# Loading q and k in 2-KB pieces and turning them with 64x64 products: chunked attention and a cosine router on one Trainium2 core

## The chip, the cores and the metric

The kernel runs on one core of one Trainium2 chip. The metric is the device time of one execution in microseconds (us); less is better. The time before is the median of three executions. A separate execution was profiled, and every line of a profile below comes from it.

## What is computed

Everything is in 32-bit floating point. The first part is attention within chunks of 64 tokens, for 8 batches, 8 heads, 576 tokens (9 chunks) and a head width of 64:

```python
q_c = q.reshape(B, H, nc, 64, D); k_c, v_c = ...
scores = matmul(q_c, k_c.transpose(0, 1, 2, 4, 3)) / sqrt(D)
attn = exp(scores - max(scores))
attn = attn / (sum(attn) + 1e-9)
out = matmul(attn, v_c)
```

Its result, 4608 tokens of 512 numbers (the 8 heads side by side), goes into a mixture of 8 experts. A router takes the cosine of each token with 8 expert vectors, divides it by tau, and sends the token to the best expert alone, with the softmax weight of that expert as a gate:

```python
logits = normalised(x) @ normalised(expert_emb).T / tau
e = argmax(logits); g = softmax(logits)[e]
out = g * (relu(x @ w1[e]) @ w2[e])        # w1: 512 x 1024, w2: 1024 x 512
```

## The kernel before

**Two parts.** The first part does attention and routing, and writes each token's row, with its place number, square sum and gate, to a table in DRAM (`spots`) at a place sorted by expert. The second part reads that table in blocks of 128 rows and runs the two layers of the experts (`hidden_part`, `result`, L196 to L250). The change touches the first part alone. It ends some 205 us into the execution.

**Tiles and rounds.** The first part works on 36 tiles of 128 tokens, that is two chunks each. A tile passes through stages: `load_qk`, `turn_qk`, `scores`, `weights`, `turn_a`, `values`, `turn_x`, `logits`, and for each four tiles `copy_logits`, `pick`, `gates`, `place` and `put`. The loop at L779 is a software pipeline whose order is written out by hand (`manual_schedule`): in the round t it emits `turn_a(t)`, `turn_qk(t+3)`, `load_qk(t+7)`, `logits(t-2)`, `scores(t+2)`, `turn_x(t-1)`, `values(t)` and `weights(t+2)`. Each engine runs its own instructions in the order in which they were emitted; semaphores between the engines do the rest. So on TensorE (PE) a round is: turn a, turn k and q, logits, scores, turn x, values.

**Loading and turning q and k.** `load_qk` (L358) brings a tile of k and of q into SBUF with one token per partition and the 8 heads side by side, 512 numbers. In DRAM the heads of a token are not neighbours, so a piece of the transfer is one head of one token, 64 numbers or 256 bytes. Tiles that lie across two batches take two transfers. q is issued by GpSimd (POOL); k by SyncE (SP) for the first four tiles and by POOL for the others. Four buffers each let the loads run four rounds ahead. `turn_qk` (L387) turns 128x128 blocks, each two heads wide, with PE's transpose into a PSUM bank: four for k, four for q. The bank of k is copied to SBUF by ScalarE (ACT, L395), that of q by VectorE (DVE, L397). The result holds the head width on partitions, even heads on the lower 64, odd ones on the upper 64, with 128 tokens along the row.

**PSUM.** The pool `ps_t` has three buffers of one bank. `turn_a`, the turn of k, the turn of q and `turn_x` take them in turn, four in a round. `scores` (L408) and `values` (L448) have two banks each of their own, and multiply by quadrants: the 64 rows of an even or odd head, against the 64 columns of one chunk or the other.

**Other names.** ACT's work in a round is the copy of aT (L436), of kxT (L395), of xT (L479), a square sum (L482) and the exponential (L428). DVE's is the copy of qxT, the maximum (L416), the subtraction (L418), and dividing by the sum (L456 to L459), which writes the token rows `xr`; there are eight buffers of these. `put` (L611) sends a row tile to `spots` with an indirect transfer issued by POOL. `load_v` (L376) brings v of a batch, 256 bytes a piece, in eight transfers on SP; the first half of batch 0 is issued by POOL.

Of the kernel before, what the change touches and what calls it, by code (L numbers as in the profile page):

```python
# [9 lines left out]
FP32 = mybir.dt.float32  # L10
# [8 lines left out]
P = 128  # L19
CH = 64  # L20
# [5 lines left out]
def kernel(  # L26
# [11 lines left out]
    nc = tc.nc  # L38
    B, H, S, Dh = q.shape
# [3 lines left out]
    NPAIR = H // 2  # L43
# [215 lines left out]
    with (  # L259
# [97 lines left out]

        def load_qk(t):  # L358

            for src, nm, eng in (  # L360
                (k, "kx", nc.sync if t < 4 else nc.gpsimd),
                (q, "qx", nc.gpsimd),
            ):
                x = qk_p.tile([P, H, Dh], FP32, tag=nm, name=nm)
                done = 0
                while done < P:
                    b, s = divmod(t * P + done, S)
                    n = min(P - done, S - s)
# [4 lines left out]
                    done += n  # L373
                qk_t[nm, t] = x.rearrange("p h d -> p (h d)")
# [12 lines left out]
        def turn_qk(t):  # L387
            for nm in ("kx", "qx"):
                a = qk_t.pop((nm, t))
                ps = ps_t.tile([P, NPAIR, P], FP32, tag="tr", name="tr")  # L390
                for i in range(NPAIR):
                    nc.tensor.transpose(ps[:, i], a[:, i * P : i * P + P], ident)  # L392
                x = wk.tile([P, NPAIR, P], FP32, tag=nm + "T", name=nm + "T")
                if nm == "kx":
                    nc.scalar.copy(x, ps)  # L395
# [532 lines left out]
```

## Time and profile before

| what | value |
|---|---|
| time, median of 3 | 737.42 us (736.25 to 737.46) |
| span of the profiled execution | 732.1 us |
| PE busy | 687.4 us, 94% |
| DVE, ACT, POOL busy | 235.2, 175.9, 167.8 us |
| mean granted clock of TensorE | 0.977 |
| DMA moved | 132.60 MB in 106,929 packets |
| packets under 512 bytes | 50,516 |

The profile names engines: PE is the matrix product, PEld its weight load, and each product in 32-bit floating point stands in it as two loads and two products. A line such as L392 is a line of the kernel; `tr<-ident,kx` names the tiles written and read; `128x512 f32` is partitions by elements. "Idle before" is the time for which the engine had nothing, and the name after the arrow is what ended it. Engines overlap, so busy times don't add up to the span: what counts is which engine has no hole in the stretch that one looks at. PE can be busy and yet not at its peak, since the profile shows a product until its results have come out.

### The profile page before, as it was taken

The page shows a single profiled execution, that of the slowest core. Times are in us where ns is not written, and L with a number is a line of the kernel's source. Part 1 is how long each engine was busy: PE and PEld are TensorE (multiplying, and loading weights), DVE is VectorE, ACT ScalarE, POOL GpSimd, SP SyncE. Part 2 cuts the span into 40 slices and gives each one's busy share as a digit, 9 for nine tenths or more (in the row PEclk, how much of TensorE's full clock was granted, in tenths as well). Part 3 has the DMA queues.
Part 4 walks back from the last instruction along what each step waited for, and adds up shares of the span by engine and source line. Part 5 has one row for each costly group of instructions (what it writes and reads, how often), then busy time and mean ns, then how long its engine had stood idle before and what let it go on. Part 6 is the DMA issues. An engine that isn't in the chain of part 4 may idle for free.

```text
span 732.1 us, 24309 instructions
## 1 busy us (share of the span) xinstructions
PE 687.4 (94%) x10327; PEld 466.1 (64%) x10327; DVE 235.2 (32%) x571; ACT 175.9 (24%) x342; POOL 167.8 (23%) x243
## 2 busy tenths in 40 slices
PE   4789999898979999999999999998999999999995
PEld 3679898797734555545545545544577777777761
DVE  2468887777553121211211211211121121121100
ACT  3356666555301111111111111111111111111110
POOL 7637776762440000001001001000000000010010
PEclk9899999899899999999999999999999999999998
DMA  9999999998946711115785416788751264411340
GB/s 199 202 185 191 255 237 241 207 230 296 351 136 246 266 54 43 36 42 201 254 324 178 162 44 219 274 323 313 273 199 43 75 233 157 151 46 41 135 165 20
DMA packets 106929, 132.60 MB, mean 181 GB/s; under 512 B 50516, under 2 KB 70996, under 8 KB 106816
## 3 DMA queue, kind: packets, MB, share of 16 engines
q1 hardware_dynamic: 94800, 93.31, 42.6%
q0 software_dynamic: 11984, 37.67, 18.2%
q8 instruction: 83, 1.36, 0.8%
q14 instruction: 30, 0.25, 0.1%
q10 hardware_dynamic: 32, 0.02, 0.0%
HBM read 341.13 MB, written 21.73 MB: 496 GB/s over the span
## 4 chain that ended last, share of the span: by engine, by line
issue 47%; PE 34%; DMA 9%; POOL 5%; DVE 4%; POOLq 0%; ACT 0%; DVEq 0%; ACTq 0%
PE h_ps L212 13%; PE y_ps L232 11%; DMA spots<-xr,dest 5%; POOL out_dram L241 3%; PE rt_ps L489 2%; DMA qx<-in_q_dram 2%; PE tr L477 2%; PE tr L392 2%; PE pv L448 2%; PE sc L408 2%; PE tr L434 1%; DMA xin<-spots 1%; DMA v<-in_v_dram 1%; DVE xr L459 1%; POOL qx L369 1%
## 5 line engine op out<-in xcount | busy, mean ns | idle before, releaser
L212 PE MATMUL h_ps<-w,xbT 128*32 128x256 f32 x4736 | 276.8, 380 | 6.6 <-issue 3.9
L232 PE MATMUL y_ps<-w,hT 128*32 128x512 f32 x2368 | 274.0, 594 | 3.5 <-DMA w<-in_moe_w_dram 2.6
L212 PEld LDWEIGHTS h_ps<-w,xbT 128*32 128x32 f32 x4736 | 203.1, 110 | 77.8 <-issue 15.1
L232 PEld LDWEIGHTS y_ps<-w,hT 128*32 128x32 f32 x2368 | 118.6, 110 | 133.4 <-issue 88.8
L222 DVE STREAM_TRANSPOSE hT<-h 128x512 f32<-128x512 f32 x74 | 52.6, 711 | 413.8 <-ACT h L221 412.7
L241 POOL DMA_INDIRECT out_dram<-y,spot x37 | 36.0, 972 | 471.7 <-ACT y L240 444.4
L221 ACT ACTIVATE h<-h_ps 128x512 f32<-128x512 f32 x74 | 44.3, 598 | 217.6 <-PE h_ps L212 217.6
L240 ACT ACTIVATE y<-y_ps,spot 128x512 f32<-128x512 f32 x37 | 25.4, 687 | 238.5 <-PE y_ps L232 219.6
L611 POOL DMA_INDIRECT spots<-xr,dest x36 | 37.4, 1039 | 45.5 <-issue 24.2
L188 DVE STREAM_TRANSPOSE xbT<-xin 128x256 f32<-128x256 f32 x74 | 43.2, 621 | 0.1
L489 PEld LDWEIGHTS rt_ps<-enT,xT 128*128 128x128 f32 x288 | 36.4, 198 | 3.7 <-DVE full L597 2.4
L489 PE MATMUL rt_ps<-enT,xT 128*128 128x8 f32 x288 | 36.3, 253 | 2.3 <-DVE full L597 2.1
L479 ACT COPY xT<-tr 128x512 f32<-128x512 f32 x36 | 21.1, 586 | 61.2 <-PE tr L477 54.6
L369 POOL DMA_DIRECT2D qx<-in_q_dram x40 | 34.4, 863 | 5.5 <-PE tr L392 2.6
L369 POOL DMA_DIRECT2D kx<-in_k_dram x36 | 31.6, 881 | 14.6 <-PE tr L392 14.2
L392 PE MATMUL tr<-ident,qx 128*128 128x128 f32 x144 | 24.5, 298 | 8.2 <-DMA qx<-in_q_dram 8.2
L392 PE MATMUL tr<-ident,kx 128*128 128x128 f32 x144 | 24.7, 299 | 7.2 <-DMA kx<-in_k_dram 6.4
L448 PE MATMUL pv<-v,aT 64*64 64x65 f32 x1152 | 28.9, 238 | 2.5 <-issue 2.4
L397 DVE COPY qxT<-tr 128x512 f32<-128x512 f32 x36 | 24.5, 681 | 17.6 <-PE tr L392 17.5
L408 PE MATMUL sc<-kxT,qxT 64*64 64x64 f32 x1152 | 27.9, 238 | 1.6 <-issue 1.5
L416 DVE TENSOR_REDUCE mx<-sc 128x8 f32<-128x512 f32 x36 | 24.7, 687 | 12.3 <-PE sc L408 9.0
L448 PEld LDWEIGHTS pv<-v,aT 64*64 64x64 f32 x1152 | 23.0, 146 | 8.2 <-issue 8.2
(140 smaller groups left out, 389.8 us busy)
## 6 DMA issues: line engine op xcount, KB each, us to landing
w<-in_moe_w_dram SPq DMA_DIRECT2D x142, 2048.0 KB
xin<-spots SPq DMA_DIRECT2D x160, 64.0 KB
qx<-in_q_dram POOLq DMA_DIRECT2D x32, 256.0 KB
v<-in_v_dram SPq DMA_DIRECT2D x56, 144.0 KB
kx<-in_k_dram POOLq DMA_DIRECT2D x28, 256.0 KB
w<-in_moe_w_dram ACTq DMA_DIRECT2D x2, 2048.0 KB
spot<-spots SPq DMA_DIRECT2D x80, 4.0 KB
spots<-blank SPq DMA_DIRECT2D x2, 528.0 KB
```

The lines of the kernel that those rows point to most:

```text
L188: nc.vector.transpose(xT[:, :, cols].rearrange("p c (b i) -> p b c i", i=Q), t[:, s * (D // 2) : (s + 1) * (D // 2)].rearrange("p (b i c) ...
L212: nc.tensor.matmul(ps[Q * r : Q * r + Q, b].rearrange("p (k i) -> p k i", i=Q), lhsT=d["xT"][:, c, t0 : t0 + Q], rhs=w[:, c, r], start=(c ...
L221: nc.scalar.activation(h, ps, AF.Relu)
L222: nc.vector.transpose(hT[:, :, G * s : G * s + G].rearrange("p k (b i) -> p b k i", i=Q), h.rearrange("p b (k i) -> p b k i", i=Q),)
L232: nc.tensor.matmul(ps[Q * r : Q * r + Q], lhsT=d["hT"][:, c, Q * r : Q * r + Q], rhs=w2_sb[r // 2][buf_of(j)][:, c], start=(c == 0), stop= ...
L241: ins = nc.gpsimd.indirect_dma_start(out=out, out_offset=bass.IndirectOffsetOnAxis(ap=spot[:, j, TOK : TOK + 1].bitcast(I32), axis=0), in_ ...
L369: eng.dma_start(out=x[done : done + n], in_=src[b, :, s : s + n, :].rearrange("h p d -> p h d"),)
L392: nc.tensor.transpose(ps[:, i], a[:, i * P : i * P + P], ident)
L408: nc.tensor.matmul(sc[CH * c : CH * c + CH, par, i], lhsT=qx[r0 : r0 + CH, i, c0 : c0 + CH], rhs=kx[r0 : r0 + CH, i, c0 : c0 + CH], start= ...
L448: nc.tensor.matmul(pv[CH * c : CH * c + CH, par, i], lhsT=d["aT"][r0 : r0 + CH, i, CH * c : CH * c + CH], rhs=v_t[b][r0 : r0 + CH, i, cb, ...
L489: nc.tensor.matmul(rt_ps[:, batch_of[t][0] % 2, batch_of[t][1]], lhsT=d["xT"][:, c], rhs=enT[:, c], start=(c == 0), stop=(c == KD - 1),)
L611: ins = nc.gpsimd.indirect_dma_start(out=spots, out_offset=bass.IndirectOffsetOnAxis(ap=at, axis=0), in_=m, in_offset=None, bounds_check=S ...
```

## The change

q and k are loaded with one head and eight neighbouring tokens per partition. Eight tokens of a head are neighbours in DRAM, so a piece is 8 x 64 numbers, or 2 KB, instead of 256 bytes; there are an eighth as many of them. A tile's two chunks are two transfers, 64 partitions each (8 heads by 8 groups of eight tokens). All k loads are issued by SP, and all of v too.

The layout in SBUF is now such that partition (h, g) holds the tokens 8g to 8g + 7 of head h. The turn takes one of the eight tokens at a time: 64 partitions by 64 numbers are the stationary operand, and 32 columns of the unit matrix, those of the even or the odd heads, are the moving one. The product puts the head width on partitions and (pair of heads, g) along the row, on the lower or upper 64 partitions for even or odd heads. For each of k and q that makes 8 tokens x 2 x 2 chunks = 32 products. A PSUM bank belongs to a chunk and holds k in its first half and q in its second. The copies to SBUF put the tokens back in order, and there are two for k and two for q, one from each bank. What later stages read is as before. The aim is to relieve the DMA engines of small pieces.

```diff
-            for src, nm, eng in (
-                (k, "kx", nc.sync if t < 4 else nc.gpsimd),
-                (q, "qx", nc.gpsimd),
-            ):
-                x = qk_p.tile([P, H, Dh], FP32, tag=nm, name=nm)
...
+            for src, nm, eng in ((k, "kx", nc.sync), (q, "qx", nc.gpsimd)):
+                x = qk_p.tile([P, H * Dh], FP32, tag=nm, name=nm)
+                for c in range(2):
+                    b, cb = divmod(2 * t + c, NCB)
                     eng.dma_start(
-                        out=x[done : done + n],
-                        in_=src[b, :, s : s + n, :].rearrange("h p d -> p h d"),
+                        out=x[CH * c : CH * c + CH],
+                        in_=src[b, :, CH * cb : CH * cb + CH, :].rearrange(
+                            "h (g j) d -> h g (j d)", j=H
+                        ),
                     )
...
         def turn_qk(t):
-            for nm in ("kx", "qx"):
+
+            banks = [
+                ps_t.tile([P, 2, 8, NPAIR, 8], FP32, tag="tr", name="tr") for c in range(2)
+            ]
+            for n, nm in enumerate(("kx", "qx")):
                 a = qk_t.pop((nm, t))
-                ps = ps_t.tile([P, NPAIR, P], FP32, tag="tr", name="tr")
-                for i in range(NPAIR):
-                    nc.tensor.transpose(ps[:, i], a[:, i * P : i * P + P], ident)
+                for j in range(8):
+                    for par in range(2):
+                        for c in range(2):
+                            r = slice(CH * c, CH * c + CH)
+                            nc.tensor.matmul(
+                                banks[c][CH * par : CH * par + CH, n, j],
+                                lhsT=a[r, j * Dh : j * Dh + Dh],
+                                rhs=ident[r, r].rearrange("p (i r g) -> p r i g", r=2, g=8)[:, par],
+                                start=True,
+                                stop=True,
+                            )
                 x = wk.tile([P, NPAIR, P], FP32, tag=nm + "T", name=nm + "T")
-                if nm == "kx":
-                    nc.scalar.copy(x, ps)
-                else:
-                    nc.vector.tensor_copy(x, ps)
+                for c in range(2):
+                    to = x[:, :, CH * c : CH * c + CH].rearrange("p i (g j) -> p i g j", j=8)
+                    came = banks[c][:, n].rearrange("p j i g -> p i g j")
+                    if nm == "kx":
+                        nc.scalar.copy(to, came)
+                    else:
+                        nc.vector.tensor_copy(to, came)
                 qkT[nm, t] = x
...
-        load_v(0, 0, 4, nc.gpsimd)
+        load_v(0, 0, 4)
```

More of the change, by code (lines that the diff above doesn't have):

```diff
@@ L358, in load_qk @@
         def load_qk(t):
-            for src, nm, eng in (
-                (k, "kx", nc.sync if t < 4 else nc.gpsimd),
-                (q, "qx", nc.gpsimd),
-            ):
-                x = qk_p.tile([P, H, Dh], FP32, tag=nm, name=nm)
[L365 to L368, printed above, removed]
+            for src, nm, eng in ((k, "kx", nc.sync), (q, "qx", nc.gpsimd)):
+                x = qk_p.tile([P, H * Dh], FP32, tag=nm, name=nm)
+                for c in range(2):
+                    b, cb = divmod(2 * t + c, NCB)
                     eng.dma_start(
-                        out=x[done : done + n],
-                        in_=src[b, :, s : s + n, :].rearrange("h p d -> p h d"),
-                    )
-                    done += n
-                qk_t[nm, t] = x.rearrange("p h d -> p (h d)")
+                        out=x[CH * c : CH * c + CH],
+                        in_=src[b, :, CH * cb : CH * cb + CH, :].rearrange(
+                            "h (g j) d -> h g (j d)", j=H
+                        ),
+                    )
+                qk_t[nm, t] = x
         def load_v(b, c0=0, c1=NCB, eng=nc.sync):
```

## The prediction

> **What bounds the kernel now.** I read the busy slices first, then stretches of the attention stage, then one round on PE and one on ACT, then the waits.
>
> ```profile
> PE   4789999898979999999999999998999999999995
> PEclk9899999899899999999999999999999999999998
> DMA  9999999998946711115785416788751264411340
> DMA packets 106929, 132.60 MB, mean 181 GB/s; under 512 B 50516, under 2 KB 70996, under 8 KB 106816
> ```
> One slice is 18.3 us. Slices 1 to 11 are attention and routing, from slice 12 on PE is full with the experts, which the change leaves alone. In slices 1 to 9 the DMA engines are full as well: half of all packets are under 512 bytes.
>
> ```profile
> 55.00:73.00 18.00, 17.94 (x370) 16.54 (x368) 14.63 (x42) 11.75 (x27) 12.75 (x18) 1.00 0.99 191
> 128.00:146.00 18.00, 15.77 (x326) 13.91 (x322) 13.60 (x38) 9.00 (x21) 12.69 (x18) 0.91 1.07 207
> ```
> Columns: PE, PEld, DVE, ACT, POOL busy, clock, DMA share, GB/s. In a good stretch PE is the bound; in a bad one it idles 2 us and loses clock.
>
> ```profile
> 65.00 0.69 PE L408 MATMUL sc<-kxT,qxT 64*64 64x64 f32 x32
> 65.62 0.66 PE L477 MATMUL tr<-ident,xr 128*128 128x128 f32 x4
> 66.21 0.69 PE L448 MATMUL pv<-v,aT 64*64 64x65 f32 x32
> 66.84 0.66 PE L434 MATMUL tr<-ident,a 128*128 128x128 f32 x4
> 67.33 0.60 PE L392 MATMUL tr<-ident,kx 128*128 128x128 f32 x4
> 67.76 0.60 PE L392 MATMUL tr<-ident,qx 128*128 128x128 f32 x4
> 68.20 0.96 PE L489 MATMUL rt_ps<-enT,xT 128*128 128x8 f32 x8
> 69.09 0.33 PE L408 MATMUL sc<-kxT,qxT 64*64 64x64 f32 x5
> ```
> One undisturbed round of a tile: 69.09 - 65.00 = 4.09 us with no hole. The two L392 turns take 0.44 us each. Over the stage a round takes more: L436 starts at 21.2 us (tile 0) and 180.7 (tile 33), 33 rounds of 4.83 us; these are the rounds that matter, since the round of tile t turns q and k of tile t + 3, and there is none to turn after tile 32. So 33 x 0.74 = 24 us are lost to waits and to half clock.
>
> ```profile
> 66.32 0.58 ACT L479 COPY xT<-tr 128x512 f32<-128x512 f32 x1 [0.87 <-PE tr L477]
> 66.80 0.63 ACT L482 ACTIVATE junk<-xr 128x512 f32<-128x512 f32 x1
> 67.33 0.19 ACT L482 ACTIVATION_READ_ACCUMULATOR junk<-xr 128x1 f32 x1
> 67.42 0.62 ACT L428 ACTIVATE a<-a 128x512 f32<-128x512 f32 x1
> 67.94 0.57 ACT L436 COPY aT<-tr 128x512 f32<-128x512 f32 x1
> 68.41 0.59 ACT L395 COPY kxT<-tr 128x512 f32<-128x512 f32 x1
> ```
> ACT does six things a round, in order, without a hole once L477's bank is there; the kx copy is the last. Now nobody waits for it soon: its reader is the L408 of the next round.
>
> ```profile
> POOL xr L465 <- DMA spots<-xr,dest: 13.5, 6, 4.8
> DVE xr L459 <- DMA spots<-xr,dest: 7.4, 5, 2.3
> ```
> What the full DMA costs: token rows leave late (us, times, longest), their buffers come free late.
>
> **What the Trainium skill says.** "PSUM — Partial Sum Buffer", section "PSUM bank collisions raise a hardware error": two engines on one bank and 32-partition quadrant collide even at other columns, so bank users must be ordered. The old program gives kx and qx a bank each, so no row of the trace shows such a wait. "TensorE: Matmul & The Clock Gate", LDWEIGHTS: a load costs its columns / 1.2 ns, whatever the rows. Trace agrees: 128-column loads of L489 start 112 ns apart (107 by the page). "DMA: Bandwidth & Descriptors", Specifications: pieces under 512 B miss line rate. Agrees: 191 GB/s at a full share above; 350 GB/s at 0.97 at 183 to 201 us, when weights come in. "TensorEngine Tiling (Array Packing)", Key Properties: changing the tiling mode drains the array. Agrees: L408's 32 records are 8 groups 58 ns apart, 0.47 us, but the next line starts after 0.62, so 0.16 us a change.
>
> **The change, part by part.**
>
> 1. PE work. Per tile 8 transposes (0.87 us) go; 64 products of 64x64 weights by 32 columns come. Each f32 product is two records (L408: 1152 for 36 x 16), so 128, four quadrants at a time: 32 groups. The nearest row is L408, with 64 columns on both sides: 58 ns a group. With 32 moving columns the 64-column load still stands, so I take 58: 16 groups or 0.93 us for kx, the same for qx. Upper end: instructions. Two event waits of PE with eight records between them stand 125 ns apart, so 15.6 ns a record at most; 8 records a group then give 125 ns, 2.0 us a turn. L408 runs at 7.3 ns, but after L489 has given the sequencer time to run ahead. I add 0.1 us to the qx turn for it. Two more mode changes: 0.16 us each.
>
> 2. The new wait. Both banks now hold kx in one half and qx in the other. In the changed kernel as built, the first qx product of each bank waits for ACT's copy of kx from that bank, and the second bank's copy is the last of ACT's chain above. Behind it on PE stands the whole round: qx turn, L489, L408, L477. And L477's bank starts ACT's chain. That closes a loop:
> - kx copy ends to qx turn starts: 0.10 (as L477 after DVE's xr at 124.1)
> - qx turn 0.93 + 0.10 + change 0.16 = 1.19
> - L489 0.99, L408 0.62 (starts of loads)
> - L477 start to ACT's xT start: 66.32 - 65.62 = 0.70
> - xT start to kx start: 68.41 - 66.32 = 2.09
> - kx as two copies. 512 elements take 0.59, the 32-element exponential (L537) 0.216: slope 0.78 ns, so 256 take 0.39; queued copies start about 0.1 before their forerunner ends. 0.29 + 0.39 = 0.68.
> Sum 6.37 us. The second loop, PE's own (qx turn 1.19, L489 0.99, L408 0.62, L477 0.59, L448 0.62, L434 0.39, change 0.16, kx turn 0.93, last result 0.24, copies 0.68, 0.10), is 6.5 at its dearest and may start the copies a little later. Every fourth round adds five ranking products and a small exponential, some 0.2 us. I take **6.5 us a round**, bounds 6.0 (denser turns, copies that cost half of one) and 8.2 (2.0 us a turn, so some 2 us more on PE's own loop, less the 0.3 us that the sequencer gains in the hole).
>
> 3. DVE: two qx copies of 0.41 for one of 0.68 (L743's 32 elements take 0.18, so 1.04 ns an element); free: it idles while PE waits. Its path to the exponential (L408's end, mx 0.72, a 0.69) ends 0.3 us before ACT comes to it.
>
> 4. DMA. 73,728 pieces of 256 B (2 x 36 x 128 x 8) become 9,216 of 2 KB. The row waits above go, and most of the 24 us would, but the round is longer than any of them: nothing of it is left to collect. The kx issues leave POOL (36 x 0.88 = 32 us of its time, off the path) and join v on SP; each load is issued four rounds ahead, 26 us, so v ahead of it in the queue costs nothing. A load now has 8 heads outermost; if it used half the engines, no row of before shows it, but 18.9 MB over 210 us is 90 GB/s, under half of what the engines move now. load_v(0) moves to SP: free.
>
> 5. Ends. At the start PE is at half clock (L408 1.1 us). Before L434 of tile 0, three tiles are turned and two scored: first load 4.0, turns 6 x 1.9 (twice 0.93), five waits for copies between them of about 0.8, L408 2 x 1.1: 21.6 us, against 19.1 now. So +3, and +2 for a cold round after it. In the tail the 1.24 us stop at 182.8 and the half clock up to 191 should go: -4.
>
> Sum: 33 x (6.5 - 4.83) = +55, +5, -4: +56 us. 737.4 + 56 = **793 us**.
>
> **Rivals.**
> - *Instructions or clock bind.* The turns run at the sequencer's pace or ACT's strided copies cost more, or the holes of 0.8 us a round bring half clock as the 2.1 us stop at 139 to 142 did. Against: the queue fills during the wait. 7.2 to 8.2 us a round: 815 to 850 us.
> - *The wait is hidden.* The kx copies come early, PE work alone counts: 4.09 + 1.87 - 0.87 + 0.32 = 5.4, with ranking 5.5: 33 x 0.67 = +22, 760 us. Against: ACT's chain stands in order and the loop above has no slack.
> - *DMA relief wins.* Small products run at twice L408's density, wait hidden: 4.4 us a round, 33 x -0.43 = -14, start -5: 718 us, faster. For: full DMA in slices 1 to 9, 24 us lost. Against: L489 shows the load as the price with 8 columns moving.
>
> **How the numbers follow.** Forecast 0.65 (T 6.0 to 6.9: 776 to 806), instructions or clock 0.23, hidden wait 0.08, relief 0.04. Leaving out a tenth on each side: 770 to 838. Faster 0.04, same 0.01, slower 0.95.
>
> **What would show it.** Rounds of 6.5 us between L436's successors; a hole on PE before the first qx product of each tile, released by ACT's kx copy, some 0.8 us; 0.93 us for 64 records of a turn's weights; DMA share well under 0.9 in slices 2 to 9 and no spots waits. Wrong if PE runs from kx to qx without a hole, or if a group takes other than 58 ns.

## The result, and the profile after

The changed kernel takes **859.98 us** (median of four runs, 854.86 to 872.33) against 736.84 us for the kernel before on the same chip: a ratio of **1.167, 95% interval 1.158 to 1.176**. The direction was right; the time is 67 us above the forecast and 22 us above the upper end of its range. The chips of the experiments run the kernel before in 719 to 735 us, so they are compared by their ratio to the kernel before on their own chip; a time in us in an expectation belongs to the 737 us of this one. Executions of one kernel differ, the ratios leave out those over 1.5% above the fastest, and two profiles below (the turns apart, the turn alone) are of such a longer execution.

The busy slices and the packets of the page after, one slice being 21.5 us:

```profile
PE   6799989989999887999999999999979999999996
PEclk9865978688685899899999999999999999999999
DMA  8824554473658721751114776147885316541331
DMA packets 110101, 133.19 MB, mean 155 GB/s; under 512 B 51220, under 2 KB 71700, under 8 KB 109952
```

PE looks as full as before. The row of the granted clock doesn't: it is at 5 to 8 tenths in most slices of the first part, where the kernel before stood at 8 or 9. The DMA engines are no longer full. The count of packets under 512 bytes has **not** fallen (50,516 before).

Two stretches of the attention stage, with the columns PE, PEld, DVE, ACT, POOL busy, clock, DMA share, GB/s:

```profile
83.00:101.00 18.00, 16.26 (x520) 14.25 (x521) 8.29 (x24) 6.57 (x17) 5.83 (x10) 0.91 0.33 105
150.00:168.00 18.00, 16.17 (x385) 14.03 (x384) 7.08 (x20) 6.04 (x15) 3.49 (x6) 0.59 0.43 110
```

PE is busy for the same 16.2 us in both, but starts 520 records of products in one and 385 in the other (the number in brackets). The second stretch runs at a clock of 0.59.

One undisturbed round at full clock, PE's rows:

```profile
96.10 0.66 PE L445 MATMUL tr<-ident,a 128*128 128x128 f32 x4
96.68 1.14 PE L394 MATMUL tr<-ident,kx 64*64 64x32 f32 x64
98.30 1.40 PE L394 MATMUL tr<-ident,qx 64*64 64x32 f32 x64 [0.48 <-ACT kxT L406]
99.63 1.06 PE L500 MATMUL rt_ps<-enT,xT 128*128 128x8 f32 x8
100.62 0.69 PE L419 MATMUL sc<-kxT,qxT 64*64 64x64 f32 x32
101.24 0.66 PE L488 MATMUL tr<-ident,xr 128*128 128x128 f32 x4
101.83 0.69 PE L459 MATMUL pv<-v,aT 64*64 64x65 f32 x32
102.45 0.66 PE L445 MATMUL tr<-ident,a 128*128 128x128 f32 x4
```

From turn a (96.10) to turn a (102.45) are 6.35 us, or 6.36 by the instructions' own starts. The forecast was 6.5. Such rounds are rare: of the 33 only four run at full clock throughout, and of those this one alone has no further stop. The new wait is there, in the brackets: PE has nothing for 0.48 us until ACT's copy of k frees the bank. On ACT the same moment looks like this:

```profile
97.20 0.57 ACT L447 COPY aT<-tr 128x512 f32<-128x512 f32 x1
97.87 0.65 ACT L406 COPY kxT<-tr 128x256 f32<-128x256 f32 x2
101.93 0.59 ACT L490 COPY xT<-tr 128x512 f32<-128x512 f32 x1 [3.42 <-PE tr L488]
```

The two copies of k stand 0.65 us. ACT then idles 3.42 us, so it is PE's own loop that sets the round.

A round at half clock, 37 us earlier:

```profile
59.02 1.11 PE L445 MATMUL tr<-ident,a 128*128 128x128 f32 x4
60.06 1.93 PE L394 MATMUL tr<-ident,kx 64*64 64x32 f32 x64
62.47 2.20 PE L394 MATMUL tr<-ident,qx 64*64 64x32 f32 x64 [0.47 <-ACT kxT L406]
64.60 1.87 PE L500 MATMUL rt_ps<-enT,xT 128*128 128x8 f32 x8
...
69.59 1.12 PE L445 MATMUL tr<-ident,a 128*128 128x128 f32 x4
```

The same work takes 69.59 - 59.02 = 10.57 us here; the wait for ACT is as long as at full clock, and PE's own rows are 1.6 to 1.8 times as long.

And a third thing, a stop in the middle of a turn:

```profile
111.85 1.04 PE L394 MATMUL tr<-ident,qx 64*64 64x32 f32 x38 [0.48 <-ACT kxT L406]
114.09 1.06 PE L394 MATMUL tr<-ident,qx 64*64 64x32 f32 x26 [1.20 <-issue]
```

"issue" means that PE waited for nothing that the profile shows. In the trace, a fetch of instructions (the queue that the profile calls "instruction", 16 KB a packet) ended at 112.67, and the products went on at 114.09. These fetches go with PE's work: in 33 rounds the kernel before has 23 of them and the change 55. Some fifteen stops of 0.4 to 2.1 us stand in the stage, counted as starts of PE that come later than is usual at their place and for which the profile names no releaser. Eight of them, with 9 of their 14 us, end 1.2 to 1.6 us after the end of a fetch; in the run below with the logits between the turns all 26 do, at 1.2 to 1.7 us.

**Where the 127 us of the two profiled spans went** (859.5 - 732.1). Measured from the copy of aT of tile 0 to that of tile 33:

| | before | after |
|---|---|---|
| aT of tile 0 at | 21.2 us | 25.9 us |
| 33 rounds | 159.5 us, 4.83 each | 279.3 us, 8.46 each |
| of these at half clock | 19.0 us, 12% | 136.5 us, 49% |
| instruction fetches in them | 23 | 55 |
| from there to the end | 551.4 us | 554.3 us |

The record of the clock begins with its first rise to full. Ahead of that the transposes of a turn start 213 ns apart, as they do at half clock (109 at full), so that time is counted as half clock, here and below.

Start +4.7, rounds +119.8, rest +2.9. Of the rounds after, 33 x 6.36 = 210 us are full-clock rounds. At half clock a round of 10.57 loses 1 - 6.36 / 10.57 = 0.40 of its time, so 136.5 us at half clock cost 54 us; the stops cost 14. Together 278 of the 279 us. Against the mean round of before, the change of round that was forecast accounts for 33 x (6.36 - 4.83) = 50 us of the loss, the clock for 54, the stops for 14.

### The profile page after: what moved, and what is told of

Same layout as the page of the kernel before. It is cut to its first block, busy times and chain, and to the rows that moved or that the text cites. A ratio compares the mean times of both kernels' runs of the same rounds, so it can differ in the third digit from the quotient of the medians.

```text
span 859.5 us, 33235 instructions
## 1 busy us (share of the span) xinstructions
PE 803.4 (93%) x14647; PEld 518.0 (60%) x14647; DVE 242.4 (28%) x607; ACT 181.0 (21%) x378; POOL 141.0 (16%) x231
## 2 busy tenths in 40 slices
DMA packets 110101, 133.19 MB, mean 155 GB/s; under 512 B 51220, under 2 KB 71700, under 8 KB 109952
## 4 chain that ended last, share of the span: by engine, by line
issue 56%; PE 34%; POOL 4%; ACT 2%; DVE 1%; DMA 1%; POOLq 0%; SPq 0%; ACTq 0%; DVEq 0%
PE tr L394 13%; PE rt_ps L500 5%; POOL out_dram L241 4%; PE sc L419 4%; PE pv L459 4%; PE tr L488 3%; PE tr L445 3%; PE h_ps L212 2%; ACT kxT L406 2%; DMA xin<-spots 1%; DMA kx<-in_k_dram 1%; POOLq L241 0%; ACT a L439 0%; DVE mx L427 0%; DVE a L429 0%
## 5 line engine op out<-in xcount | busy, mean ns | idle before, releaser
L232 PE MATMUL y_ps<-w,hT 128*32 128x512 f32 x2368 | 265.3, 596 | 3.5 <-DMA w<-in_moe_w_dram 2.8
L212 PEld LDWEIGHTS h_ps<-w,xbT 128*32 128x32 f32 x4736 | 182.1, 111 | 101.9 <-issue 32.1
L232 PEld LDWEIGHTS y_ps<-w,hT 128*32 128x32 f32 x2368 | 91.2, 111 | 156.4 <-issue 146.9
L394 PE MATMUL tr<-ident,qx 64*64 64x32 f32 x2304 | 62.1, 241 | 25.5 <-ACT kxT L406 18.7
L394 PEld LDWEIGHTS tr<-ident,qx 64*64 64x64 f32 x2304 | 54.2, 158 | 33.3 <-ACT kxT L406 22.9
L364 POOL DMA_DIRECT2D qx<-in_q_dram x72 | 42.5, 597 | 146.2 <-PE tr L394 144.8
L394 PE MATMUL tr<-ident,kx 64*64 64x32 f32 x2304 | 53.2, 246 | 7.1 <-DMA kx<-in_k_dram 6.0
L408 DVE COPY qxT<-tr 128x256 f32<-128x256 f32 x72 | 27.3, 420 | 108.3 <-PE tr L394 105.9
L394 PEld LDWEIGHTS tr<-ident,kx 64*64 64x64 f32 x2304 | 48.3, 165 | 15.8 <-issue 10.4
L500 PE MATMUL rt_ps<-enT,xT 128*128 128x8 f32 x288 | 45.4, 285 | 0.0
```

The costliest lines, as they stand in the source:

```text
L212: nc.tensor.matmul(ps[Q * r : Q * r + Q, b].rearrange("p (k i) -> p k i", i=Q), lhsT=d["xT"][:, c, t0 : t0 + Q], rhs=w[:, c, r], start=(c ...
L232: nc.tensor.matmul(ps[Q * r : Q * r + Q], lhsT=d["hT"][:, c, Q * r : Q * r + Q], rhs=w2_sb[r // 2][buf_of(j)][:, c], start=(c == 0), stop= ...
L364: eng.dma_start(out=x[CH * c : CH * c + CH], in_=src[b, :, CH * cb : CH * cb + CH, :].rearrange("h (g j) d -> h g (j d)", j=H),)
L394: nc.tensor.matmul(banks[c][CH * par : CH * par + CH, n, j], lhsT=a[r, j * Dh : j * Dh + Dh], rhs=ident[r, r].rearrange("p (i r g) -> p r ...
L500: nc.tensor.matmul(rt_ps[:, batch_of[t][0] % 2, batch_of[t][1]], lhsT=d["xT"][:, c], rhs=enT[:, c], start=(c == 0), stop=(c == KD - 1),)
```

## The experiments

Three theories for the clock and the stops had to be told apart. **HOLE**: PE's stops for the copy of k, half a microsecond or more each round, bring half clock, as the forecast's rival had it. **SUPPLY**: 416 products and loads a round (the 32 products of a turn are two records each, with a load for every record: 128 for k, 128 for q) are more than the fetches bring in time. **ACTIVITY**: too few columns are in motion. The turns load 64 columns of weights to move only 32, so PE is busy with loading while little moves.

For ACTIVITY I work out how long columns move in a round at full clock: columns times 0.83 ns (an estimate: transposes of 128 columns start 109 ns apart at full clock, 0.85 ns a column with the step from one to the next), times two records for a product that isn't a transpose, divided by the number of quadrant products that run side by side. After: turn a and turn x 0.43 each, scores and values 0.43 each, logits 0.05, the turns of k and q 0.43 each, 2.62 us of 6.36. The kernel before has the same 2.62 us, in 4.09.

### One at a time: the moving columns, the number of products

**The change with 64 moving columns.** Nothing but the width of the moving operand differs, and results of neighbouring products overlap, so the output isn't the reference's:

```diff
-                                banks[c][CH * par : CH * par + CH, n, j],
+                                banks[c].rearrange("p n j i g -> p n (j i g)")[
+                                    CH * par : CH * par + CH, n, 32 * min(j, 6) : 32 * min(j, 6) + CH
+                                ],
                                 lhsT=a[r, j * Dh : j * Dh + Dh],
-                                rhs=ident[r, r].rearrange("p (i r g) -> p r i g", r=2, g=8)[:, par],
+                                rhs=ident[r, r],
```

Expected: 

> The changed kernel with 64 moving columns (all of the chunk's unit matrix) instead of 32 in each of the 64 products of a tile; a product overwrites the second half of its neighbour's columns, so q and k come out partly wrong. Instructions, waits, copies and the weight loads that set the pace (58 ns a group of four) stay; the array has twice the columns in motion. Theory ACTIVITY (few moving columns read as an idle array and bring half clock): half clock falls from 49% of the stage to under 15%, a round 7.0 to 7.3 us, 1.08 to 1.11 of before. Theory SUPPLY (stops for want of instructions bring half clock): half clock stays at 40 to 50%, 1.15 to 1.18 of before.

**Half as many products.** 128 rows of weights (both chunks) by 64 columns, 64 columns moving: 16 products a tensor in place of 32. The two banks are split by odd and even j, so the wait and the two copies stay. The copies and the operands of the scores follow the new layout (left out here).

```diff
-                        for c in range(2):
-                            r = slice(CH * c, CH * c + CH)
-                            nc.tensor.matmul(
-                                banks[c][CH * par : CH * par + CH, n, j],
-                                lhsT=a[r, j * Dh : j * Dh + Dh],
-                                rhs=ident[r, r].rearrange("p (i r g) -> p r i g", r=2, g=8)[:, par],
+                        nc.tensor.matmul(
+                            banks[j % 2][CH * par : CH * par + CH, n, j // 2],
+                            lhsT=a[:, j * Dh : j * Dh + Dh],
+                            rhs=ident.rearrange("p (m r g) -> p r m g", r=2, g=8)[:, par],
...
```

Expected: 

> The changed kernel with half as many products in the turn: 16 of 128 rows by 64 weight columns by 64 moving columns for each of k and q instead of 32 of 64 by 64 by 32. Same weight load time at full clock (0.93 us a turn), k and q still share two banks (now even and odd tokens of the eight), so the wait for the copies of k and the two copies each stay. 288 instead of 416 instructions a round. HOLE: half clock stays at 45 to 50%, about 840 us. SUPPLY: fewer fetches (55 in 33 rounds down to some 38) and stops, half clock 20 to 30%, a round 6.6 to 7.2 us, 795 to 815 us. ACTIVITY: twice the columns in motion, half clock under 15%, about 790 us.

**Half as many products, 32 moving columns.** The same, with half of the unit matrix's columns left out, so half of each tile isn't turned and the copies read the other half twice. Against the kernel with half as many products:

```diff
-                            rhs=ident.rearrange("p (m r g) -> p r m g", r=2, g=8)[:, par],
+                            rhs=ident.rearrange("p (m r g) -> p r m g", r=2, g=8)[:, par, 0:4],
...
```

Expected: 

> The half-products version (16 products of 128 rows by 64 weight columns for each of k and q, wait kept, 1.073 of before, no half clock) with 32 moving columns instead of 64; half of the turned tokens are left out and the copies read the other half twice. 288 instructions a round as there. ACTIVITY: half clock comes back, over 30% of the stage, a round over 7.2 us, over 1.11 of before. SUPPLY: no half clock, a round 6.1 to 6.2 us, 1.065 to 1.08.

Measured, with the change itself, as ratio to before (interval), round, share of the 33 rounds at half clock, time in the stops without a releaser, of 0.3 us and more:

| products and loads a round, columns in the turns | ratio | round, undisturbed | round, mean | half clock | stops |
|---|---|---|---|---|---|
| 416, 32 (the change) | 1.167 (1.158 to 1.176) | 6.36 us | 8.46 us | 49% | 14 us |
| 416, 64 | 1.135 (1.128 to 1.143) | 6.41 | 7.57 | 16% | 20 us |
| 288, 32 | 1.172 (1.162 to 1.181) | 6.12 | 8.23 | 66% | none |
| 288, 64 | 1.073 (1.067 to 1.079) | 6.18 | 6.15 | **0%** | none |

The same 110 us of the four, in the order of the table, one row of a stretch from each trace:

```profile
40.00:150.00 110.00, 100.37 (x2699) 87.22 (x2692) 47.20 (x134) 37.71 (x92) 28.95 (x50) 0.75 0.46 118
```
```profile
40.00:150.00 110.00, 97.90 (x3115) 84.30 (x3109) 55.30 (x156) 43.04 (x108) 34.74 (x59) 0.93 0.57 140
```
```profile
40.00:150.00 110.00, 105.71 (x1973) 92.64 (x1974) 52.25 (x149) 39.97 (x99) 32.35 (x55) 0.70 0.52 135
```
```profile
40.00:150.00 110.00, 103.64 (x2582) 89.77 (x2579) 66.74 (x194) 50.04 (x127) 44.04 (x73) 1.00 0.75 177
```

Read the third and the fourth together. PE is busy for 105.71 us in the one and 103.64 in the other, so the one with *less* idle time has the clock of 0.70, the other 1.00. The undisturbed rounds are as long as each other (6.12 and 6.18), since the load of the weights sets the pace and not the columns that move. What differs is the columns. That is ACTIVITY, twice: at 416 products and loads (49% to 16%) and at 288 (66% to 0%). Both runs with 288 came out as ACTIVITY had said. The one with 416 and 64 columns came within a point of it in the clock (under 15% expected), but not in the time (1.08 to 1.11 expected), since its stops grew. HOLE falls: the wait is in all four. These are PE's waits for ACT's copy in the whole execution (us, times, longest) of the change, of half the products, and of half the products with 32 columns:

```profile
PE tr L394 <- ACT kxT L406: 18.7, 36, 1.4
PE tr L392 <- ACT kxT L404: 15.0, 36, 1.3
PE tr L392 <- ACT kxT L405: 11.7, 36, 0.4
```

The second has no half clock, and the third, with the shortest waits, has the most. SUPPLY is another matter: in these four the stops come with 416 products and loads and are gone with 288, at either width, and taking them away alone gives nothing (1.172). The number in a round isn't all of it, though: the kernel before, with 176, has nine stops of 0.3 to 1.7 us, 7 us in all.

### The wait, the logits, and work in the hole

**Own banks.** Half as many products again, with a bank for k and one for q, hence no wait between the turns and one copy each. Against the kernel with half as many products:

```diff
-            banks = [
-                ps_t.tile([P, 2, 4, CH], FP32, tag="tr", name="tr") for c in range(2)
-            ]
+                ps = ps_t.tile([P, 8, CH], FP32, tag="tr", name="tr")
...
-                            banks[j % 2][CH * par : CH * par + CH, n, j // 2],
+                            ps[CH * par : CH * par + CH, j],
...
```

Expected: 

> As the half-products version, but k has a bank of its own and q another: no wait of q's turn for k's copy, and one copy each as before the change. All theories: hole and most stops go, so half clock under 15% and a round 5.4 to 5.7 us (4.09 of before, less 0.87, plus two turns of 0.93 and two mode changes): 755 to 770 us. If half clock stays over 30%, none of HOLE and SUPPLY is the cause.

Measured: 1.043 (1.038 to 1.049), an undisturbed round of 5.43 us against 6.18, half clock 0%, as expected. Without the wait seven stops of 0.4 to 1.7 us are back, 6 us in all. The shared banks, with the second copy that they need, are worth 0.75 us a round and 3% of the time, where the clock doesn't interfere. This is the best that a turn of this kind did here, and still 4% slower than before.

**Logits between the turns.** The change, with `logits(t-2)` emitted between the turn of k and that of q, so that PE has work while ACT copies k:

```diff
...
-                turn_qk(t + 3)
-                if t + 7 < NT:
-                    load_qk(t + 7)
+                turn_qk(t + 3, 0)
             if 0 <= t - 2 < NT:
                 logits(t - 2)
             if t - 2 in ends:
                 copy_logits(ends[t - 2])
+            if t + 3 < NT:
+                turn_qk(t + 3, 1)
```

Expected: 

> The changed kernel with the logits of a round (0.99 us of TensorE work) emitted between the turn of k and the turn of q, so that they fill the hole in which TensorE waits for the copies of k. Nothing else moves; two more mode changes (0.3 us). Theory HOLE (the wait's hole brings the clock to half): half clock falls from 49% of the stage to under 15%, a round is 5.7 to 6.0 us instead of 8.46, time 770 to 780 us. Theory SUPPLY (the stops of 0.5 to 1.5 us within bursts, where instructions are missing, bring half clock): the stops stay, half clock stays near 40%, a round 7.3 to 7.8 us, time 820 to 840 us. Theory ACTIVITY (products with 32 moving columns count as too little work): half clock stays near 50%, about 840 us.

Measured: 1.131 (1.121 to 1.141). The waits for ACT's copy fall from 18.7 to 2.5 us in all and an undisturbed round is 5.41 us:

```profile
PE tr L398 <- ACT kxT L410: 2.5, 5, 0.5
```

Half clock is still there in 39% of the rounds' time, and the stops cost 30 us, so the mean round is 7.57. Hardly a hole, and yet the clock falls: HOLE alone can't be it. The numbers are those that SUPPLY had foretold, so by itself this run doesn't decide between SUPPLY and ACTIVITY; the four of the table do.

**Useless work in the hole.** The change, with 16 products between the two turns whose results nobody reads, 128 columns moving in each:

```diff
...
+                if n == 0 and t > 0:
+                    ps = ps_s.tile([P, 2, 512], FP32, tag="sc", name="sc")
+                    sc_ps[t - 1] = ps
+                    for i in range(4):
+                        for par in range(2):
+                            for c in range(2):
+                                r = slice(CH * par, CH * par + CH)
+                                nc.tensor.matmul(
+                                    ps[CH * c : CH * c + CH, par, 256 + P * (i % 2) :][:, 0:P],
+                                    lhsT=ident[r, r],
+                                    rhs=ident[r, :],
...
```

Expected: 

> After, with useless work in the hole: between the turn of k and that of q of a tile, 16 products of 64x64 weights by 128 columns of the unit matrix (32 records, 8 groups of some 107 ns, 0.85 us) go into columns of the scores' banks that nothing reads. Nothing else is changed, so PE has more to do. HOLE (PE's stops of 0.5 us bring half clock) and ACTIVITY (too few columns in motion bring it) both say that half clock becomes rarer, from 49% of the stage to 0 to 25%; a round at full clock becomes 6.36 - 0.475 + 0.85 = 6.75 us plus the two changes of size, up to 6.9, and the kernel comes out faster than the change itself although it does more: 1.08 to 1.14 of before. By ACTIVITY the share of a round with columns moving is (2.62 + 0.85) / 6.75 = 51%, at the bound, so half clock should be rare but not gone. SUPPLY (the stops after instruction fetches are what starts it) says no gain: 448 products a round in place of 416 need more fetches, half clock stays at 45% or more, and 33 rounds x 0.4 to 0.8 us make it slower than the change: 1.18 to 1.22.

```profile
116.88 1.19 PE L396 MATMUL tr<-ident,kx 64*64 64x32 f32 x64
117.90 1.07 PE L410 MATMUL sc<-ident 64*64 64x128 f32 x32
118.80 1.16 PE L396 MATMUL tr<-ident,qx 64*64 64x32 f32 x64
119.89 1.06 PE L516 MATMUL rt_ps<-enT,xT 128*128 128x8 f32 x8
```
```profile
40.00:150.00 110.00, 99.23 (x3379) 89.20 (x3372) 52.01 (x149) 40.66 (x101) 31.24 (x54) 0.92 0.50 126
```

Measured: half clock falls from 49% to 22% and the clock of this stretch rises from 0.75 to 0.92, as ACTIVITY said. The time stays at 1.170 (1.163 to 1.177), which it did not: the stops grow from 14 to 33 us, 0.6 us a round more. An undisturbed round lasts 6.36 to 6.8 us. So the 0.85 us of useless work bought back some 0.40 x 78 = 31 us of clock, and lost as much in stops and in the work itself. My expectation had left the longer supply of instructions out of the sum.

### Order alone

The granted clock in the records changes on a grid of 3.41 us. The Trainium skill, "TensorE: Matmul & The Clock Gate", Part 1, has such a window, free-running, with half rate after an idle one and full rate after a busy one; the runs agree on the 3.41 us. I worked out how long columns moved in each such window (weighted with the part of the array that a product covers). In the change, 16 of 41 full-clock windows were followed by half clock, 14 of which moved columns for at most 0.25 of their time; of the 25 that kept the clock three did. So it seemed that a thin stretch longer than a window was to blame: turn of k, hole, turn of q and logits, 3.8 us in a row. Two orders were to test that.

**Logits after the scores**, which makes the thin stretch 2.8 us:

```diff
-            if 0 <= t - 2 < NT:
-                logits(t - 2)
-            if t - 2 in ends:
-                copy_logits(ends[t - 2])
             if t == NT:
                 turn_x(t - 1)
             early_parts(t, 0)
             if 0 <= t + 2 < NT:
                 scores(t + 2)
+            if 0 <= t - 2 < NT:
+                logits(t - 2)
+            if t - 2 in ends:
+                copy_logits(ends[t - 2])
```

Expected: 

> After, with the logits (8 moving columns, 0.99 us) emitted after the scores in place of between the turn of q and the scores. Same products, same wait, same hole of 0.5 to 0.7 us between the turns; only the order on PE differs, and two changes of size fall away. ACTIVITY with windows: the granted clock in the traces changes on a grid of 3.4 us, and it falls after a window in which columns moved for less than about 0.26 of it (worked out: columns x 0.83 ns x rows x columns of the tile / 128 / 128). In the changed kernel turn of k, hole, turn of q and logits stand in a row for 3.8 us and move columns for 0.95 us: a whole window at 0.26 to 0.28. With the logits moved the thin stretch is 2.8 us, and the thinnest window holds 0.85 + 0.43 us, 0.37 of it. So half clock no longer starts by itself, only after a stop for instructions: 5 to 25% of the stage in place of 49%, a round of 6.6 to 7.5 us, 1.09 to 1.14 of before. If only the mean over a round counts (2.62 / 6.2 = 42%, hardly changed), half clock stays at 40 to 50% and the time at 1.155 to 1.175.

Measured: 1.190 (1.179 to 1.200), undisturbed round 6.13 us, half clock 48%. **A miss.** Less work of PE (two changes of size), and no gain at all.

**The turns apart**, in the order turn a, turn of k, scores, turn x, turn of q, values, logits:

```diff
...
+                turn_qk(t + 3, 0)
...
             if 0 <= t + 2 < NT:
                 scores(t + 2)
             if 0 <= t - 1 < NT - 1:
                 turn_x(t - 1)
+            if t + 3 < NT:
+                turn_qk(t + 3, 1)
             if 0 <= t < NT:
                 values(t)
+            if 0 <= t - 2 < NT:
+                logits(t - 2)
```

Expected: 

> After, with the turns apart: in a round PE does turn a, turn of k, scores, turn x, turn of q, values, logits, so thin work (the turns, the logits) alternates with dense work, and ACT's copy of k has scores and turn x to hide in. Same products. HOLE gone: no idle time of PE before the turn of q that ACT's kx copy ends. Window rule: the thinnest 3.4 us at full clock (logits, turn a, turn of k, half of scores) move columns for 1.3 us, 0.39: half clock starts only after a stop. But once it is there, the same stream at half clock holds about 0.26 to 0.37 in a window, and traces show the clock come back only above about 0.35 to 0.4, so it can then last long. Expected: PE's full-clock round 5.5 to 5.8 us, half clock 5 to 35% of the stage, 6.2 to 7.5 us a round with stops, 1.06 to 1.13 of before. If half clock follows the mean over a round (2.62 / 5.6 = 47%), 30 to 40% as in the run with the logits between the turns, 1.12 to 1.14.

Measured: 1.141 (1.131 to 1.151), undisturbed round 5.78 us, no wait for ACT's copy, half clock in 48% of the rounds' time. The time is above the range of the window rule and at the upper end of what the mean over a round gives; the half clock is above both. Spreading the thin work has two sides. Fewer windows fall under the lower mark by themselves, but the stops of up to 3.8 us still push some there; and once at half clock, the evened stream has few windows dense enough to bring the clock back. In the change, windows at half clock with under 0.33 never brought it back and those over 0.38 always did. In the two new orders most half-clock windows lie between 0.19 and 0.35. There the clock fell 9 times in the recorded part of the rounds in place of 16, but then stayed down for 15 us (logits after the scores) and 12 us (turns apart) in the mean, against 8.5 in the change. That last reading is from the records and wasn't tried by itself.

Taken over the rounds of all fourteen traces, the windows show both marks. Of the windows at full clock, 64 of the 66 with under 0.24 of moving columns were followed by half clock, 25 of the 39 from 0.24 to 0.28, and 1 of the 438 with 0.38 or more. Of those at half clock, none of the 116 under 0.28 brought the clock back, and 55 of the 56 with 0.38 or more did. PE's busy time tells less: in 30 of the 101 windows after which the clock fell PE was busy for 85% or more. So the windows go a long way to say when the clock falls and returns; what the forecasts of the two orders missed is how long it stays down. These marks were read off afterwards, and no run was made to test them.

Over the runs, half clock goes with the share of the undisturbed round in which columns move (the kernel before has its 12% from windows in which PE stood waiting, with 0.11 to 0.24 of moving columns):

| kernel | moved / round | share | half clock |
|---|---|---|---|
| before | 2.62 / 4.09 us | 64% | 12% |
| half products, own banks | 3.47 / 5.43 | 64% | 0% |
| half products, 64 columns | 3.47 / 6.18 | 56% | 0% |
| work in the hole | 3.47 / 6.36 | 55% | 22% |
| the change, 64 columns | 3.47 / 6.41 | 54% | 16% |
| logits between | 2.62 / 5.41 | 48% | 39% |
| turns apart | 2.62 / 5.78 | 45% | 48% |
| half products, 32 columns | 2.62 / 6.12 | 43% | 66% |
| logits after scores | 2.62 / 6.13 | 43% | 48% |
| the change | 2.62 / 6.36 | 41% | 49% |

From 54% up half clock takes 22% of the time at most, from 48% down 39% at least. Within the two groups the share doesn't order the runs.

### The loads and the turn apart from each other

**The loads alone**: 2-KB pieces and k on SP, with the turn as it was before. The tokens then stand in the wrong order, so the output isn't the reference's; all transfers and all work are there.

```diff
...
-                x = qk_p.tile([P, H, Dh], FP32, tag=nm, name=nm)
...
+                x = qk_p.tile([P, H * Dh], FP32, tag=nm, name=nm)
+                for c in range(2):
...
+                        in_=src[b, :, CH * cb : CH * cb + CH, :].rearrange(
+                            "h (g j) d -> h g (j d)", j=H
+                        ),
...
```

Expected: 

> The 2-KB loads of the changed kernel with the turn of before (8 transposes of 128x128 a tile, one bank each): the tokens of q and k come out in the wrong order, all counts and sizes are those of before. What the relief of the DMA engines is worth alone: row waits on spots go, DMA share in the stage falls under 0.7, a round 4.2 to 4.5 us instead of 4.83, and the start some 5 us earlier: 710 to 725 us. If DMA was hidden anyway: 733 to 740 us.

Measured: 1.0007 (0.9977 to 1.0037), 4.70 us a round. No gain, as expected for DMA time that is hidden. Why, the profile's queues show; first those of before, then those of this run (packets, MB, share of 16 engines' span):

```profile
q1 hardware_dynamic: 94800, 93.31, 42.6%
q0 software_dynamic: 11984, 37.67, 18.2%
```
```profile
q1 hardware_dynamic: 98000, 102.22, 47.3%
q0 software_dynamic: 11920, 28.77, 12.6%
```

POOL's transfers are in q0. In the kernel before, 12 thousand packets carried 37.67 MB, 3.1 KB each: q and k, whose pieces are 256 bytes, had travelled there in packets of 4 KB (the trace has them so, at 14.7 GB/s an engine) all along. The packets under 512 bytes are mostly those that SP issues, of v above all: 38,912 of 256 bytes, at 9.3 GB/s an engine. k moved from the one queue to the other as 2-KB packets at 20.3 GB/s. These rates are bytes over the packets' own time, from 40 to 150 us. In the same stretch the DMA engines' share went from 1.03 to 0.93 at 222 and 229 GB/s: 10% relief where the forecast counted on eightfold fewer pieces.

**The turn alone**: the change's turn on the loads of before (again with tokens in the wrong order).

```diff
-            for src, nm, eng in ((k, "kx", nc.sync), (q, "qx", nc.gpsimd)):
+            for src, nm, eng in (
+                (k, "kx", nc.sync if t < 4 else nc.gpsimd),
+                (q, "qx", nc.gpsimd),
+            ):
...
```

Expected: 

> The turn of the changed kernel on the loads of before (256 bytes a piece, k on POOL from tile 4 on); the tokens of q and k come out in the wrong order, counts and sizes are the same. If all of the loss is the turn: 1.15 to 1.19 of before, as the whole change. SUPPLY: a fuller DMA slows the fetch of instructions, so rather at or above the upper end. If the loads in 2 KB cost or bring something in the changed kernel, it is the distance from 1.167.

Measured: 1.192 (1.183 to 1.200), at the upper end of the forecast; a round takes 9.06 us, and half clock 63% of it. So the turn is the whole loss. Beside it the loads may be worth 2%, which isn't shown: this run and the change itself were compared on different chips.

**All of v issued by POOL**, on the kernel before, to have v's small pieces in large packets too:

```diff
-        def load_v(b, c0=0, c1=NCB, eng=nc.sync):
+        def load_v(b, c0=0, c1=NCB, eng=nc.gpsimd):
```

Expected: 

> The kernel before with all loads of v issued by POOL instead of SP, nothing else. In the trace of before POOL's loads move in packets of 4 KB at 16 GB/s an engine, SP's loads of v in packets of 256 B at 9. If the small packets of v are what fills the DMA engines, their time in the stage falls by 16%, the row waits on spots shrink, 0.97 to 0.99 of before. If POOL's own queue is the bound (0.6 us for each of 64 issues more, on an engine that is 70% busy), the rows leave later: 1.00 to 1.02.

Measured: 1.036 (1.030 to 1.042), slower than either forecast. The packets under 512 bytes do fall, to 15,701, and the DMA share of the stretch to 0.71. But the issues take POOL 51.5 us, and they stand in front of its arithmetic. Waits of DVE and PE, in us, times and longest:

```profile
DVE rn L525 <- POOL rn L524: 21.8, 5, 6.1
```
```profile
PE tr L392 <- DVE qxT L397: 15.7, 4, 4.7
```

DVE waits for POOL's norm, the copy of q waits behind that on DVE, and PE stops for 3.0 to 4.7 us before a turn, four times. A load of k makes it wait 8.5 us more, once, at the start of the stage. Half clock takes 28% of the rounds' time. DMA relief on the wrong queue turned into a wait.

**Twelve buffers of token rows in place of eight**, on the kernel before, an attempt at something faster than both:

```diff
-        NX = 2 * RB
+        NX = 3 * RB
```

Expected: 

> Before, with twelve in place of eight buffers of token rows (xr), and nothing else: an attempt at something that beats both kernels, by taking away what the profile of before names as waits on spots (13.5 us on POOL, 7.4 us on DVE). If those waits are what costs the 24 us by which 33 rounds of before are longer than 33 undisturbed ones, the time falls by 5 to 15 us, to 0.98 to 0.993. If they lie beside PE's work, or if the full DMA engines are the cause and the buffers only move the wait, it stays within 0.5%.

Measured: 0.9945 (0.9922 to 0.9967). The rows of waits of `xr` for `spots` are gone from the profile (13.5 and 7.4 us before), but the gain is 4 us, between the two forecasts: the DMA engines are as full as before (1.01 of the stretch from 40 to 150 us, 1.03 before), and most of those waits lay beside PE's work. It is the only version here that beats both kernels, by half a per cent.

## Why the prediction was wrong

**Step 1, the turns' work: right.** A turn of k takes 0.92 us from the first to the last start (0.93 predicted), one of q 1.18 (1.03 with the supply's 0.10, before the change of size). The supply has no part in that: 0.27 us lie between the first product of q and the second, which goes to the other bank and starts 0.05 us after ACT's second copy ends (98.52); the rest runs at k's pace. The group's 58 ns hold: the load of 64 columns is the price, not the 32 that move. The upper end of 15.6 ns a record didn't occur as a steady pace.

**Step 2, the wait: right in place, kind and size.** From the last product of k to the second of q are 0.97 us; the forecast had 0.24 + 0.68 + 0.10 = 1.02. The profile shows it in two pieces, a hole of 0.48 us and the 0.27 after the first product. ACT's idle 3.42 us shows that of the two loops PE's own set the round: 6.36 us measured, 6.5 at its dearest. The bounds 6.0 to 8.2 were those of a round at full clock, and the mean of 8.46 lies above even the dearest.

**Step 3, DVE and ACT: right.** The copies of q take 0.42 us (0.41), the two of k 0.65 together (0.68), and PE doesn't wait for the copies of q.

**Step 4, DMA: wrong in its premise, harmless in the sum.** The count of pieces in DRAM was taken for the count of packets. POOL's queue had carried them in 4-KB packets already, so the packets under 512 bytes stayed (50,516 and 51,220). The row waits did shrink, but not through the loads: with the loads alone POOL's were 19.8 us, in the change 4.4, with longer rounds that ask for less in a microsecond:

```profile
POOL xr L476 <- DMA spots<-xr,dest: 4.4, 1, 4.4
```

**Step 5, ends: start right (+5, measured +4.7); tail wrong** (-4 predicted, +2.9 measured).

**The step that failed is the sum, 33 x (6.5 - 4.83).** It multiplied an undisturbed round by 33. For the kernel before, the same profile had shown what that leaves out: an undisturbed round of 4.09 against a mean of 4.83. The forecast treated that difference as the price of full DMA engines, which would go, and gave the new stream full clock throughout. It fell to half clock for 49% of the rounds' time: 54 us that no term of the sum held. Another 14 us went into stops for instructions, which step 1 had priced as 0.1 us a round and which are 14 / 33 = 0.42.

That the kernel is slower, and the round of 6.36 us, were foreseen by the right mechanism and aren't luck; but one round in 33 runs like that. The rival "Instructions or clock bind" is what happened, with both of its halves, but at 8.46 us above its 7.2 to 8.2. And it named the wrong trigger. The holes don't bring half clock: the kernel with half the products has holes of 0.37 us in its rounds and none of it, and with half as many moving columns in the same products 66%. The evidence was in step 1 itself, which says that 64 columns are loaded to move 32: PE's time for the turns doubles while what it moves stays. It served for the price of a product, and what it means for the clock wasn't asked.

Left open: what the clock's control counts (the shares are worked out, and in these runs more columns in motion always mean more multiplications too) and how long it stays at half, which no rule of single windows that I tried predicts; and why a fetch is followed by a stop, which was only seen in its timing. It grows with the number of products in the runs with shared banks, but the kernel before has some of it with the fewest.

## What to carry to other kernels

When a change replaces dense products by small ones, work out for how much of a round columns move, before and after, beside PE's busy time: here under half meant half clock for two fifths to two thirds of the time, with PE 90% busy in the change (251.9 of 279.3 us). A product whose weights take longer to load than its columns to move can be widened for almost nothing (6.36 to 6.41 us an undisturbed round for twice the columns), and with fewer, larger products the stops after fetches went as well (20 us to none at 64 columns). Before relieving the DMA engines of small pieces, look which queue the small packets are in: those of POOL's queue weren't small, whatever the access pattern said.

## What the runs showed of the hardware

- Half clock without idleness. The Trainium skill, "TensorE: Matmul & The Clock Gate", Part 1, puts half rate down to idle windows. The run with 288 products and loads and 32 columns had PE busy for 105.71 of 110 us and a clock of 0.70.
- Clock and useless work: 0.85 us of products a round that nobody reads raised the clock of a stretch from 0.75 to 0.92.
- The Trainium skill, "Runtime: NRT & Kernel Launch", Instruction fetch mechanics, calls the fetch mostly hidden. Here stops of PE stand behind fetches: 14 us in 33 rounds of the change (416 products and loads in 6.36 us), 20 with 64 columns, none with 288 in 6.18 us, but 7 us in the kernel before (176 in 4.09 us).
- Pieces of 256 bytes, neighbours in SBUF, travelled as packets of 4 KB when POOL issued them and as packets of 256 bytes when SP did: 14.7 and 9.3 GB/s an engine.
